# Weights ahead of the small value loads, bf16 masks, zero products and an earlier list: the opening of a fused attention and gated FFN kernel

## Chip, cores and metric

The kernel runs on one core of a Trainium2 chip. The metric is the device time of one launch in microseconds (us). Three runs of the kernel before took 1149.44, 1150.88 and 1152.57; the median is 1150.88.

## What is computed

The input is q, k and v of 8 batches, 8 heads, 576 positions and 64 dimensions, and the weights of a gated FFN. The attention has two parts that are added: a coarse one over means of four positions, and a local one over a band of seven keys. The sum is normalised and goes through the FFN.

```python
def _attn_ref(q, k, v):
    ...
    q_d = q.reshape(B, H, Sd, factor, D).mean(axis=3)
    ...
    out_d = sm_attn(q_d, k_d, v_d)
    out_up = np.repeat(out_d, factor, axis=2)
    mask = np.abs(pos[:, None] - pos[None, :]) < factor
    scores = scale * np.matmul(q, k.transpose(0, 1, 3, 2))
    scores = np.where(mask, scores, -1000000000.0)
    ...
    return (out_up + out_local).astype(np.float32)

def _moe_ref(x, w_gate, w_val, w_out, rms_g):
    rms = np.sqrt(np.mean(x * x, axis=-1, keepdims=True) + 1e-06)
    xn = x / rms * rms_g
    g = xn @ w_gate
    silu = g * (1.0 / (1.0 + np.exp(-g)))
    val = xn @ w_val
    return (silu * val @ w_out).astype(np.float32)
```

There are 4608 tokens of 512 features, and the FFN is 1536 wide. The weights arrive as 64-bit floats.

## The kernel before

The tokens go in 18 chunks of 256. Products on TensorE (PE) are made of two parts, a high and a low one, so a product of the FFN takes three matmuls.

**FFN of a chunk.** `Forward` goes through 12 slices f of 128 hidden features. The first step of a slice (L1323, 24 matmuls of 128x256) multiplies the normalised tokens xh and xl with w_gate and w_val. ACT takes the tanh (L1331), DVE makes the gate (L1334) and the product (L1339), ACT the high part (L1345), DVE or POOL the low part (L1348). The second step (L1359, 6 matmuls of 128x512) multiplies with w_out; it runs two slices behind the first.

**Local attention of a chunk c.** From c = 2 on it is `Attention`: eight pairs of score product (L786) and score sum (L790) on DVE, a softmax (L807 to L824), value products on ACT (L833), POOL and DVE (L840) with a sum on DVE (L859), the addition of the coarse part (L868, L874), squares (L884), the mean on PE (L891), the norm on DVE (L923), a turn on PE (L935), and the high and low part of the turned tokens (L940, L944), with which chunk c's FFN can start. For c = 0 and 1 it is `Dense`: masked scores on PE (the mask by an identity product L1089, the scores L1103), a softmax (L1118 to L1139), turns (L1145, L1156), values (L1166), the coarse part (L1178 for chunk 0; for chunk 1 loaded with L1188 and added with L1193), squares (L1205), the norm (L1235, L1237), the turn (L1247), the high part (L1250) and the low part (L1254). Its values come with `load_v`, 72 small transfers of v (L1072 of up to 16x512 elements, L1080 smaller).

**Coarse attention.** It goes in pieces: scores (L521), peak on DVE (L531), exps on ACT (L541), turn on PE (L550), copies on ACT (L558), values on PE (L565), scaling on DVE (L579) and a store to memory that ACT issues (L582). Eight pieces stand in the opening, the others beside the later chunks. Their sums over four positions come by a load on SP (L356, L360) and adding transfers of POOL (L364).

**Weights.** They come in 36 pieces of 512 KB. Each is fetched by SP (L251), scaled on ACT (L255), its last bits are taken on POOL (L265), both are joined on DVE (L272), the high part is made on ACT (L282, L284) and the low part split off on DVE (L294, L296) or POOL (L292). The fetches go to a few buffers that are used in turn, so a fetch waits until the piece before it in its buffer is joined.

**Order.** `Plan` (L66 to L160) is a list scheduler: tasks have an engine, a cost, a due time and buffers, and where several tasks could start on an engine at about the same time the one that is due first goes first. With it the opening is written out, from the first load to the last product of chunk 0's FFN, all weight pieces among it. Everything behind it comes from a loop over c = 1 to 17: it emits chunk c's FFN and between its slices the steps of chunk c + 1's attention, and the tile scheduler places these instructions, also between those of the opening. Each engine executes its instructions in the order that results. The transfers that SP and ACT issue share eight completion semaphores, and a transfer waits for the one before it on its semaphore.

Of the kernel before, what the change touches and what calls it, by code (L numbers as in the profile page):

```python
# [41 lines left out]
FIRST = 1  # L42
PIECES = {1: (0, 3, 6), 2: (0, 3, 6), 3: (0, 2)}
# [126 lines left out]
def attn_moe_kernel(  # L170
# [439 lines left out]
    class Attention:  # L610


        def __init__(self, c, na=4, np_=2, on_tensor=None):
            self.c, self.na, self.np, self.pt = c, na, np_, on_tensor
            self.x, self.qk, self.v, self.pr, self.y, self.up = {}, {}, {}, {}, {}, {}

        def steps(self):
# [46 lines left out]
            todo = [(0.37 * i, lambda i=i: score(i)) for i in range(8)] + [(3.0, softmax)]  # L664
# [4 lines left out]
        def plan(self, newton="POOL", before=()):  # L669
            c, np_, on_tensor, T = self.c, self.np, self.pt, due[self.c]  # L670
            early = c == 0
            sc, r = buf("sc"), buf("rms")
            xs, ups = [buf("x_t") for _ in range(2)], [buf("up_t") for _ in range(2)]
            self.xh_buf, self.xl_buf = buf("xh"), buf("xl")
            tps = [buf("ps_a") for _ in range(2)]

            loaded, k_bufs, last = {}, {}, []
            for n, jp in enumerate(jps):
                k_bufs[jp] = buf("kv"), buf("sil" if early and n > 1 else "q_t")
                loaded[jp] = task(  # L680
                    "SP", 0.15, lambda jp=jp: self.load_score(*jp), T - 88 + 7 * n - (200 if early else 0), allocs=k_bufs[jp],
                    dma=0.448 * MB,
                )
            for i, (j, par, s0) in enumerate(trio):
                at = T - 70 + 3.6 * i
                pr = buf("prod")
                p = task(
                    "DVE", 1.1, lambda i=i: self.score(i), at, [loaded[j, par]],
                    allocs=[pr] + ([sc] if i == 0 else []), uses=[*k_bufs[j, par], sc],
                )  # L690
                last.append(task("DVE", 1.08, lambda i=i: self.score_sum(i), at + 0.1, [p, *last[-1:]], uses=[pr, sc]))

            at = T - 40
            t = task("DVE", 0.5, self.peak, at, last, uses=[sc])
            t = task("DVE", 0.27, self.less, at, [t], uses=[sc])
            t = task("ACT", 0.3, self.powers, at, [t], uses=[sc])
            t = task("DVE", 0.26, self.total, at, [t], uses=[sc])
            t = task("DVE", 0.42, self.invert, at, [t], uses=[sc])
            shares = task("DVE", 0.27, self.shares, at, [t], uses=[sc])

            v_loaded, v_bufs, made = {}, {}, []
            for n, jp in enumerate(jps):
                v_bufs[jp] = buf("kv")
                v_loaded[jp] = task(
                    "SP", 0.1, lambda jp=jp: self.load_value(*jp), T - 55 + 7 * n - (60 if early else 0), allocs=[v_bufs[jp]],
                    dma=0.32 * MB,
                )
            self.y_bufs = [buf(on_tensor[1]) for _ in range(2)] if on_tensor else []
            for i, (j, par, s0) in enumerate(trio):
                at = T - 38 + 2.8 * i  # L710
                pr = buf("prod")
                first = task(
                    "ACT", 0.25 * self.na, lambda i=i: self.value_scalar(i, 0), at, [shares, v_loaded[j, par]],
                    allocs=[pr], uses=[v_bufs[j, par], sc],
                )
                parts = [first, task(
                    "ACT", 0.25 * self.na, lambda i=i: self.value_scalar(i, 1), at, with_=[first], uses=[pr, v_bufs[j, par], sc],
                )]
                for e, o0, o1, cost in (
                    ("DVE", self.na, NO - np_, 0.2 + 0.13 * (NO - np_ - self.na)), ("POOL", NO - np_, NO, 0.1 + 0.38 * np_),  # L720
                ):
                    if o0 < o1:
                        parts.append(task(
                            e, cost, lambda i=i, e=e, o0=o0, o1=o1: self.value(i, e, o0, o1), at, with_=[first],
                            uses=[pr, v_bufs[j, par], sc],
                        ))
                x0 = par == s0 == 0
                if on_tensor:
                    made.append(task(
                        "PE", 0.22 * NO, lambda i=i: self.value_sum(i), at - TAIL, [*parts, *made[-1:], *before],  # L730
                        allocs=[self.y_bufs[j]] if x0 else [], uses=[pr, self.y_bufs[j]],
                    ))
                else:
                    made.append(task(
                        "DVE", 1.07, lambda i=i: self.value_sum(i), at + 0.5, [*parts, *made[-1:]],
                        allocs=[xs[j]] if x0 else [], uses=[pr, xs[j]],
                    ))
            self.made = made

            up_ready = [stored[b, hp] for p_ in {(2 * c + j) // UPP for j in range(2)} for b in (2 * p_, 2 * p_ + 1) for hp in range(KT)]  # L740
            squares, adds = [], []
            for j in range(2):
                load = task("ACT", 0.12, lambda j=j: self.load_up(j), T - 30, up_ready, allocs=[ups[j]], lag=2.5)
                add = task(
                    "DVE", 0.69, lambda j=j: self.add_up(j), T - 18 + 3 * j, [made[4 * j + 3], load],
                    allocs=[xs[j]] if on_tensor else [], uses=[ups[j], xs[j], *([self.y_bufs[j]] if on_tensor else [])],
                )
                adds.append(add)
                squares.append(task("ACT", 1.1, lambda j=j: self.squares(j), T - 18 + 3 * j, [add], uses=[ups[j], xs[j]]))
            self.added = adds  # L750
            mp = buf("ps_a")
            mean = task("PE", 0.2, self.mean, T - 10 - TAIL, squares, allocs=[mp])
            rms = task("DVE", 0.48, self.rms, T - 10, [mean], allocs=[r], uses=[mp])
            root = task(newton, 2.6 if newton == "POOL" else 1.9, lambda: self.root(newton), T - 10, [rms], uses=[r])
            self.turned, self.turns = [], []
            for j in range(2):
                norm = task("DVE", 0.69, lambda j=j: self.norm(j), T - 8, [root], uses=[xs[j]])
                turn = task(
                    "PE", 0.6, lambda j=j: self.turn(j), T - 7 - TAIL, [norm],
# [718 lines left out]
    for b in q_bufs:  # L1478
        b.users.extend(atts[1].turns[:1])
    for n in range(len(pieces)):  # L1480
        decode(n)
# [109 lines left out]
```

## Time and profile before

| | us |
|---|---|
| profiled execution | 1153.86 |
| its span, first to last instruction | 1152.1 |
| median of three runs | 1150.88 |
| chunk 0's first FFN matmul (L1323) | 123.7 |
| chunk 0's output copies (L1367) begin | 234.3 |
| chunk 1's output copies begin | 293.6 |
| PE busy, over the span | 1053.5 |
| DVE busy | 908.7 |
| mean granted clock of PE | 0.948 |

A view of stretches has a row for each piece of time: the busy time of each engine with its number of instructions, PE's granted clock as a share of full speed, the share of time that the 16 transfer engines were busy, and the rate of transfers. A view of waits has the engine, the line that waited, what it waited for, and then the total, the number of times and the longest. A group of instructions has its line, engine, operation, names and shapes, the number, the busy time and the mean duration in ns, and the idle time before it. A row on one line gives the shortest, median and longest duration in ns and the first and last start. PEld is PE's loading of weights, which lies beside its matmuls; SPq is SP's own queue.

### The profile page before, as it was taken

How to read it: one execution, taken by the hardware profiler on the slowest of the kernel's cores; microseconds unless marked ns; L12 is line 12 of the kernel's file. 1: busy time of each engine (PE TensorE's matmuls, PEld its weight loads, DVE VectorE, ACT ScalarE, POOL GpSimd, SP SyncE). 2: the span in 40 equal slices, each digit the busy share in tenths (PEclk: the TensorE clock that was granted, in tenths of full speed). 3: DMA queues.
4: the chain of work that ended last, by engine and by line, in shares of the span. 5: the costliest groups of instructions: out<-in, count | busy, mean ns of one | idle time of the engine just before them, and what ended most of it. 6: DMA issues, size and time to landing. Idle time of an engine off the chain costs nothing.

```text
span 1152.1 us, 22708 instructions
## 1 busy us (share of the span) xinstructions
PE 1053.5 (91%) x8256; PEld 963.7 (84%) x8256; DVE 908.7 (79%) x1874; ACT 611.7 (53%) x2237; POOL 225.0 (20%) x279
## 2 busy tenths in 40 slices
PE   4285665799999999999999999999999999999998
PEld 3164554789999899999999999999999999999997
DVE  5246989736969898989898888888898989897432
ACT  3145477335556566474847474737374563837222
POOL 4122533602221213030312121101010010101000
PEclk9556687899999999999999999999999999999999
DMA  8356624832645444535353535322221313220000
GB/s 255 120 177 198 240 65 128 181 80 41 157 89 125 95 120 92 129 73 133 79 128 83 131 85 123 91 68 71 68 89 46 106 52 99 67 59 20 1 19 19
DMA packets 74172, 115.28 MB, mean 100 GB/s; under 512 B 26204, under 2 KB 34652, under 8 KB 74060
## 3 DMA queue, kind: packets, MB, share of 16 engines
q1 hardware_dynamic: 45484, 93.15, 26.6%
q0 software_dynamic: 8640, 15.93, 8.9%
q10 hardware_dynamic: 19936, 4.76, 1.9%
q8 instruction: 65, 1.06, 0.4%
q14 instruction: 47, 0.39, 0.1%
HBM read 102.00 MB, written 11.80 MB: 99 GB/s over the span
## 4 chain that ended last, share of the span: by engine, by line
PE 81%; DMA 7%; DVE 5%; SPq 3%; ACT 2%; issue 1%; POOL 1%; ACTq 0%; DVEq 0%; POOLq 0%
PE ps_h L1323 49%; PE ps_o L1359 25%; PE ps_a L565 2%; SPq L1072 2%; DMA wg<-in_v_sum_dram 2%; DMA qk<-in_qk_sum_dram 2%; PE ps_a L521 1%; PE ps_a L935 1%; PE ps_a L550 1%; ACT prod L833 1%; DVE prod L786 1%; DVE o_sb L272 1%; DMA wv<-in_w_val_dram 1%; DVE sc L790 1%; DMA up_t<-up 1%
## 5 line engine op out<-in xcount | busy, mean ns | idle before, releaser
L1359 PE MATMUL ps_o<-wo,hs 128*128 128x512 f32 x1296 | 340.5, 401 | 11.6 <-DVE hs L1348 7.5
L1323 PE MATMUL ps_h<-xh,wg 128*128 128x256 f32 x1728 | 319.2, 281 | 1.4 <-DVE wg L296 1.4
L1323 PE MATMUL ps_h<-xh,wv 128*128 128x256 f32 x1728 | 316.7, 280 | 0.0
L1323 PEld LDWEIGHTS ps_h<-xh,wg 128*128 128x128 f32 x1728 | 268.0, 190 | 10.3 <-issue 3.3
L1359 PEld LDWEIGHTS ps_o<-wo,hs 128*128 128x128 f32 x1296 | 231.6, 190 | 51.6 <-DVE hs L1348 8.4
L833 ACT ACTIVATE prod<-kv,sc 128x64 f32<-128x64 f32 x1024 | 262.4, 406 | 20.7 <-DMA up<-o_g 7.7
L1323 PEld LDWEIGHTS ps_h<-xh,wv 128*128 128x128 f32 x1728 | 268.4, 191 | 2.9 <-issue 0.4
L1323 PE MATMUL ps_h<-xl,wv 128*128 128x256 f32 x864 | 242.8, 281 | 19.9 <-DVE sil L1334 18.1
L1323 PE MATMUL ps_h<-xl,wg 128*128 128x256 f32 x864 | 244.3, 283 | 0.1
L1331 ACT ACTIVATE sil<-ps_h 128x256 f32<-128x256 f32 x216 | 81.5, 378 | 235.3 <-PE ps_h L1323 219.5
L1323 PEld LDWEIGHTS ps_h<-xl,wv 128*128 128x128 f32 x864 | 165.0, 191 | 24.2 <-DVE sil L1334 20.3
L1323 PEld LDWEIGHTS ps_h<-xl,wg 128*128 128x128 f32 x864 | 164.2, 190 | 7.2 <-DVE sil L1339 0.9
L840 POOL TENSOR_TENSOR prod<-sc,kv 128x256 f32<-128x256 f32 x128 | 96.2, 789 | 375.6 <-DVE sc L824 161.5
L859 DVE TENSOR_REDUCE x_t<-prod 128x128 f32<-128x896 f32 x128 | 136.2, 1074 | 31.1 <-PE ps_a L935 27.8
L1345 ACT ACTIVATE hs<-sil 128x256 fp32r<-128x256 f32 x216 | 89.2, 414 | 133.7 <-DVE sil L1339 104.5
L1334 DVE SCALAR_TENSOR_TENSOR sil<-sil,ps_h 128x256 f32<-128x256 f32 x216 | 88.9, 412 | 66.7 <-ACT sil L1331 64.2
L786 DVE TENSOR_TENSOR prod<-q_t,kv 128x896 f32<-128x896 f32 x128 | 140.5, 1100 | 0.1
L790 DVE TENSOR_REDUCE sc<-prod 128x14 f32<-128x896 f32 x128 | 136.9, 1073 | 0.0
L1348 DVE TENSOR_TENSOR hs<-sil,hs 128x256 fp32r<-128x256 f32 x209 | 97.2, 468 | 30.6 <-ACT hs L1345 30.0
L1339 DVE SCALAR_TENSOR_TENSOR sil<-sil,ps_h 128x256 f32<-128x256 f32 x216 | 89.6, 415 | 2.3 <-PE ps_h L1323 0.8
L364 POOL DMA_DIRECT2D qk<-in_qk_sum_dram x36 | 32.7, 907 | 250.0 <-DMA qk<-in_qk_sum_dram 207.9
L541 ACT ACTIVATE a_g<-ps_a,m_g 72x144 f32<-72x144 f32 x112 | 40.5, 370 | 38.9 <-DMA kv<-in_v_sum_dram 25.5
(169 smaller groups left out, 928.1 us busy)
## 6 DMA issues: line engine op xcount, KB each, us to landing
kv<-in_k_pad_dram SPq DMA_DIRECT2D x64, 320.0 KB
kv<-in_v_pad_dram SPq DMA_DIRECT2D x64, 320.0 KB
qk<-in_qk_sum_dram POOLq DMA_DIRECT2D x36, 288.0 KB, 5.0
out_dram<-o_sb SPq DMA_DIRECT2D x36, 256.0 KB
q_t<-in_q_band_dram SPq DMA_DIRECT2D x64, 128.0 KB
vs<-in_v_sum_dram POOLq DMA_DIRECT2D x36, 144.0 KB, 3.3
qk<-in_qk_sum_dram SPq DMA_DIRECT2D x12, 288.0 KB
wo<-in_qk_sum_dram SPq DMA_DIRECT2D x2, 1152.0 KB
```

The costliest lines, as they stand in the source:

```text
L786: nc.vector.tensor_tensor(out=pr, in0=bcast(q[:, s0:s0 + 2], 2, NO), in1=window(k, s0), op=ALU.mult)
L790: nc.vector.tensor_reduce(out=self.sc[:, j, par, s0:s0 + 2], in_=self.pr[i], axis=AX.X, op=ALU.add,)
L833: nc.scalar.activation(out=self.pr[i][:, o, s], in_=self.v[j, par][:, s0 + s + o], func=AF.Copy, scale=p[:, s, o:o + 1],)
L840: (nc.vector if engine == "DVE" else nc.gpsimd).tensor_tensor(out=self.pr[i][:, a:b], in0=bcast(p[:, :, a:b].rearrange("p s o -> p o s"), ...
L859: nc.vector.tensor_reduce(out=self.x[j][:, s0:s0 + 2, par], in_=pr.rearrange("p o s d -> p s d o"), axis=AX.X, op=ALU.add,)
L1323: last = nc.tensor.matmul(out=self.p[f][:, t], lhsT=wi(f)[:, 0, k], rhs=xi[:, k], start=(n == 0), stop=(n == 3 * KT - 1),).ins
L1331: nc.scalar.activation(out=self.sil[f], in_=self.p[f][:, 0], func=AF.Tanh, scale=0.5)
L1334: nc.vector.scalar_tensor_tensor(out=self.sil[f], in0=self.sil[f], scalar=1.0, in1=self.p[f][:, 0], op0=ALU.add, op1=ALU.mult,)
L1339: nc.vector.scalar_tensor_tensor(out=self.sil[f], in0=self.sil[f], scalar=0.5, in1=self.p[f][:, 1], op0=ALU.mult, op1=ALU.mult,)
L1345: nc.scalar.activation(out=self.hs[f][:, 0], in_=self.sil[f], func=AF.Copy)
L1348: (nc.gpsimd if engine == "POOL" else nc.vector).tensor_tensor(out=self.hs[f][:, 1], in0=self.sil[f], in1=self.hs[f][:, 0], op=ALU.subtract,)
L1359: last = nc.tensor.matmul(out=self.o[j], lhsT=lhs[:, cols], rhs=rhs(f)[:, 0], start=(f == 0 and i == 0), stop=(f == NF - 1 and i == 2),).ins
```

## The change

1. **Transfers.** The due times of `load_v` change, so that SP issues the first eight weight pieces ahead of the 72 small transfers of v.
2. **Masks.** The masks and the identity that brings them into the scores become bf16, for which POOL makes a bf16 copy of the identity; the costs of the dense scores and values in the list become smaller.
3. **Zero products.** Up to 100 products of a zero matrix (bf16, 128x256) are offered to the list for PE, due last, so that they stand where the list has PE free. They add nothing to their accumulator. Those that fall behind chunk 0's squares are not issued: 28 are.
4. **Scores of the third chunk.** `Attention.plan`, which nothing used, is removed; `plan_scores` puts the third chunk's (c = 2) key loads, score pairs and softmax into the list, due from 130 on, and the loop leaves them out.

```diff
-                        "SP", 0.25, lambda b=b, e=e: self.load_v(b, e), (-80 if early else 45) + 2 * b + e,
+                        "SP", 0.25, lambda b=b, e=e: self.load_v(b, e), (50.0 if early else 53.5) + 0.1 * (2 * b + e),
...
-                    "PE", 3.4 if b == 0 else 2.6, lambda b=b: self.scores(b), at + 2 * b,
+                    "PE", 1.8 if b == 0 else 0.9, lambda b=b: self.scores(b), at + 2 * b,
...
+                for i in range(IDLE):
+                    task("PE", 0.13, self.idle, 1e6 + i, first, not_before=20.0 + 0.3 * i)
...
-                        out=self.s[par].rearrange("p b t a k -> p (b t a) k"), lhsT=ident_sb,
+                        out=self.s[par].rearrange("p b t a k -> p (b t a) k"), lhsT=masks["ident"],
...
+        def idle(self):
+            if not hasattr(self, "ss"):
+                nc.tensor.matmul(
+                    out=self.x[0][:, 0].rearrange("p h d -> p (h d)"), lhsT=masks["zero"], rhs=bcast(masks["ident"], 1, 2),
+                    start=False, stop=True, skip_group_check=True,
+                )
...
+        masks["ident"] = t.bitcast(BF16)[:, 2 * D:2 * D + P]
+        nc.gpsimd.tensor_copy(out=masks["ident"], in_=ident_sb)
+        masks["zero"] = t.bitcast(BF16)[:, 6 * D:8 * D]
+        nc.gpsimd.memset(masks["zero"], 0.0)
...
+        def plan_scores(self, at):
+            self.scored = True
...
+                loaded[jp] = task(
+                    "SP", 0.4, lambda jp=jp: self.load_score(*jp), at - 20 + 5 * n, allocs=k_bufs[jp], dma=0.448 * MB,
+                )
+            for i, (j, par, s0) in enumerate(trio):
...
+                    "DVE", 1.1, lambda i=i: self.score(i), at + 3 * i, [loaded[j, par]],
...
+    early = Attention(2).plan_scores(130.0)
     for n in range(len(pieces)):
         decode(n)
...
-            nxt = Attention(c + 1)
+            nxt = early if c == FIRST else Attention(c + 1)
```

The rows below are the instructions of one engine in the order in which they stand, those of the changed kernel with its own line numbers. On SP, behind the loads of the sums, before the change (L1072 and L1080 are the small transfers of v, L251 the weights):

```order
L1072 DMA kv<-in_v_sum_dram 12x1x512
L1072 DMA kv<-in_v_sum_dram 16x1x512 x3
L1080 DMA kv<-in_v_sum_dram 4x4x64 x2
L1072 DMA kv<-in_v_sum_dram 16x1x512 x8
L251 DMA wg_1_359<-in_w_gate_dram 128x1024
L251 DMA wg_1_359<-in_w_val_dram 128x1024
```

The same place in the changed kernel (L252 is L251, L1001 is L1072, L1009 is L1080):

```order
L252 DMA wg_1_296<-in_w_gate_dram 128x1024
L252 DMA wg_1_296<-in_w_val_dram 128x1024
L252 DMA wg_1_328<-in_w_out_dram 128x1024
L252 DMA wg_1_328<-in_w_gate_dram 128x1024
L252 DMA wv_1_358<-in_w_val_dram 128x1024
L252 DMA wv_1_358<-in_w_out_dram 128x1024
L252 DMA wv_1_392<-in_w_gate_dram 128x1024
L252 DMA wv_1_392<-in_w_val_dram 128x1024
L1001 DMA kv<-in_v_sum_dram 12x1x512
L1001 DMA kv<-in_v_sum_dram 16x1x512 x3
```

Before, 40 small transfers of chunk 0 stand ahead of the first weight; now eight weights stand ahead of the first small one.

On DVE, behind chunk 0's low parts, before the change (L272 joins, L296 splits, L786 and L790 score pairs, L1334 gate):

```order
L296 SCALAR_TENSOR_TENSOR wv_0_861<-o_sb,g_sb,wv_0_860 128x4x128
L786 TENSOR_TENSOR prod<-q_t,kv 128x896 x2
L272 SCALAR_TENSOR_TENSOR o_sb<-o_sb,wv_1_434 128x512 x2
L272 SCALAR_TENSOR_TENSOR o_sb<-o_sb,wv_1_521 128x512
L790 TENSOR_REDUCE sc<-prod 128x14 x2
L1334 SCALAR_TENSOR_TENSOR sil<-sil,ps_h 128x256
L296 SCALAR_TENSOR_TENSOR wg_0_527<-o_sb,g_sb,wg_0_526 128x4x128
L786 TENSOR_TENSOR prod<-q_t,kv 128x896
```

In the changed kernel the first score pair (L712, L716) stands far behind, after the splits (L297) and joins (L273) of nearly all pieces (L1270 is the gate, L1275 the product, L1284 the low part):

```order
L273 SCALAR_TENSOR_TENSOR o_sb<-o_sb,wo_2_587 128x512
L297 SCALAR_TENSOR_TENSOR wv_1_1517<-o_sb,g_sb,wv_1_1516 128x4x128
L712 TENSOR_TENSOR prod<-q_t,kv 128x896
L716 TENSOR_REDUCE sc<-prod 128x14
L712 TENSOR_TENSOR prod<-q_t,kv 128x896
L1270 SCALAR_TENSOR_TENSOR sil<-sil,ps_h 128x256 x2
L273 SCALAR_TENSOR_TENSOR o_sb<-o_sb,raw 128x512
L1275 SCALAR_TENSOR_TENSOR sil<-sil,ps_h 128x256
```

Of the 36 joins all but two stand ahead of the first score; before, the scores of the third and of the fourth chunk stand between them. The fourth chunk's scores stand behind the third's in both.

On PE the zero products that stand close together are those between the scores and the turn of the eighth coarse piece. Before:

```order
L1178 MATMUL ps_o<-o_g,q_t 64x128 x2
L521 MATMUL ps_h<-xl 72x144 x4
L550 MATMUL ps_h<-ident_sb,a_g 72x72 x8
L1145 MATMUL ps_a<-ident_sb,wo_1_865 128x128 x4
L565 MATMUL ps_h<-hs,a_g 72x64 x8
```

In the changed kernel (L1107 is L1178, L1114 the zero product, L522 is L521; 18 more zero products follow the last row here, and then the turn):

```order
L1107 MATMUL ps_o<-o_g,q_t 64x128 x2
L1114 LDWEIGHTS q_t
L1114 MATMUL ps_o<-q_t 128x256
L522 MATMUL ps_h<-xl 72x144 x4
L1114 LDWEIGHTS q_t
L1114 MATMUL ps_o<-q_t 128x256
```

The first scores of the ninth coarse piece (L521, with the first sums that POOL adds) stand on PE behind chunk 1's slice 4 (16 first steps and 12 second steps of chunks 0 and 1 are ahead of them); before, 14 and a third first steps and 11 second steps are.

More of the change, by code (lines that the diff above doesn't have):

```diff
@@ L42 @@
 FIRST = 1
+IDLE = 100
 PIECES = {1: (0, 3, 6), 2: (0, 3, 6), 3: (0, 2)}
@@ L613, in __init__ @@
         def __init__(self, c, na=4, np_=2, on_tensor=None):
-            self.c, self.na, self.np, self.pt = c, na, np_, on_tensor
+            self.c, self.na, self.np, self.pt, self.scored = c, na, np_, on_tensor, False
             self.x, self.qk, self.v, self.pr, self.y, self.up = {}, {}, {}, {}, {}, {}
@@ L662, in turn @@
                 return last
-            todo = [(0.37 * i, lambda i=i: score(i)) for i in range(8)] + [(3.0, softmax)]
+            todo = [] if self.scored else [(0.37 * i, lambda i=i: score(i)) for i in range(8)] + [(3.0, softmax)]
             todo += [(3.1 + 0.42 * i, lambda i=i: value(i)) for i in range(8)]
@@ L667, in steps @@
             return todo, root, turn
[L669 to L675, printed above, removed]
+        def plan_scores(self, at):
+            self.scored = True
+            sc = buf("sc")
@@ L677, in plan @@
             loaded, k_bufs, last = {}, {}, []
             for n, jp in enumerate(jps):
-                k_bufs[jp] = buf("kv"), buf("sil" if early and n > 1 else "q_t")
+                k_bufs[jp] = buf("kv"), buf("q_t")
                 loaded[jp] = task(
-                    "SP", 0.15, lambda jp=jp: self.load_score(*jp), T - 88 + 7 * n - (200 if early else 0), allocs=k_bufs[jp],
-                    dma=0.448 * MB,
+                    "SP", 0.4, lambda jp=jp: self.load_score(*jp), at - 20 + 5 * n, allocs=k_bufs[jp], dma=0.448 * MB,
@@ L683, in plan @@
                 )
             for i, (j, par, s0) in enumerate(trio):
-                at = T - 70 + 3.6 * i
                 pr = buf("prod")
                 p = task(
-                    "DVE", 1.1, lambda i=i: self.score(i), at, [loaded[j, par]],
+                    "DVE", 1.1, lambda i=i: self.score(i), at + 3 * i, [loaded[j, par]],
                     allocs=[pr] + ([sc] if i == 0 else []), uses=[*k_bufs[j, par], sc],
                 )
-                last.append(task("DVE", 1.08, lambda i=i: self.score_sum(i), at + 0.1, [p, *last[-1:]], uses=[pr, sc]))
@@ L693, in plan @@
[L693 to L759, printed above, removed]
-                    allocs=[tps[j]] + ([self.xh_buf, self.xl_buf] if j == 0 else []), uses=[xs[j], self.xh_buf, self.xl_buf],
-                )
-                high = task("ACT", 0.58, lambda j=j: self.high(j), T - 7, [turn], uses=[tps[j], self.xh_buf])
-                low = task("DVE", 0.69, lambda j=j: self.low(j), T - 7, [high], uses=[tps[j], self.xh_buf, self.xl_buf])
-                self.turned += [high, low]
-                self.turns.append(turn)
+                last.append(task("DVE", 1.08, lambda i=i: self.score_sum(i), at + 3 * i, [p, *last[-1:]], uses=[pr, sc]))
@@ L766, in plan @@
+            t = last
+            for e, cost, f in (
+                ("DVE", 0.5, self.peak), ("DVE", 0.27, self.less), ("ACT", 0.3, self.powers), ("DVE", 0.26, self.total),
+                ("DVE", 0.42, self.invert), ("DVE", 0.27, self.shares),
+            ):
+                t = [task(e, cost, f, at + 24, t, uses=[sc])]
             return self
@@ L1014, in plan @@
                 values.append(task(
-                    "PE", 2.8, lambda par=par: self.values(par), end - 15 + par,
+                    "PE", 1.2, lambda par=par: self.values(par), end - 15 + par,
                     [copies[par], *v_ready, *values[-1:], *(first if early else [p.valued for p in pieces])],
@@ L1033, in plan @@
             self.valued = values[-1:]
+            if early:
+                for i in range(IDLE):
+                    task("PE", 0.13, self.idle, 1e6 + i, first, not_before=20.0 + 0.3 * i)
             x_ts = [buf("x_t") for _ in range(2)]
@@ L1453, in make_masks @@
         for c in range(2):
-            masks[c] = t[:, c * D:(c + 1) * D]
+            masks[c] = t.bitcast(BF16)[:, c * D:(c + 1) * D]
             nc.gpsimd.tensor_scalar(
```

## Prediction

> **What bounds the kernel now.** I read the page's head first, then the stretches of the span, then where four milestones lie.
>
> ```profile
> span 1152.1 us, 22708 instructions
> PE 1053.5 (91%) x8256; PEld 963.7 (84%) x8256; DVE 908.7 (79%) x1874; ACT 611.7 (53%) x2237; POOL 225.0 (20%) x279
> ```
>
> The stretches give the busy time of PE, PEld, DVE, ACT, POOL, then the granted clock.
>
> ```profile
> 120.00:150.00 30.00, 22.33 (x112) 19.36 (x113) 30.00 (x39) 13.65 (x29) 15.42 (x14) 0.78 0.59 202
> 150.00:180.00 30.00, 22.52 (x122) 19.73 (x121) 26.35 (x55) 25.40 (x74) 12.01 (x14) 0.83 0.24 74
> 180.00:210.00 30.00, 15.35 (x83) 13.70 (x84) 29.75 (x42) 17.55 (x58) 10.82 (x10) 0.77 0.48 147
> 210.00:240.00 30.00, 24.94 (x175) 22.82 (x174) 15.33 (x35) 12.35 (x42) 14.37 (x17) 0.94 0.82 160
> 240.00:270.00 30.00, 30.00 (x245) 27.39 (x245) 12.45 (x42) 8.94 (x32) 5.17 (x6) 1.00 0.36 62
> ```
>
> From 240 us on PE is full at clock 1.00, so only what comes earlier can change. From 120 to 210 DVE is full and PE has holes; from 210 to 270 DVE is half idle. The milestones, each the first start of its line:
>
> ```profile
> L1235 DVE TENSOR_SCALAR x_t<-ps_o,rinv x2: 473/478/482, 109.2 to 109.6; 128x256 f32<-128x256 f32 x2
> L1323 PE MATMUL ps_h<-xl,wg x864: 276/276/583, 123.7 to 1142.4; 128*128 128x256 f32 x173
> L923 DVE TENSOR_TENSOR x_t<-x_t,rinv x32: 682/686/692, 270.1 to 1085.4; 128x512 f32<-128x512 f32 x32
> L944 DVE TENSOR_TENSOR xl<-ps_a,xh x32: 678/680/703, 279.3 to 1091.7; 128x512 fp32r<-128x512 f32 x32
> ```
>
> Chunk 0's norm is at 109.2, its FFN starts at 123.7, chunk 2's norm is at 270.1 and its xl starts at 279.3; its two parts of 0.68 end near 281, when chunk 2's FFN starts. After that both kernels hold the same work (chunk 3's scores are done by then in both), on a full PE. So the change is worth what it moves the 281. What PE waited for between 120 and 240 (total, times, longest):
>
> ```profile
> PE ps_h L1323 <- DVE sil L1334: 18.1, 7, 4.5
> PE ps_a L1193 <- DMA raw<-up: 8.3, 1, 8.3
> PE ps_o L1359 <- DVE hs L1348: 7.5, 2, 5.7
> PE ps_o L1359 <- POOL hs L1348: 4.1, 2, 2.1
> PE ps_a L521 <- DMA qk<-in_qk_sum_dram: 2.0, 1, 2.0
> ```
>
> **The scores, the largest part.** DVE works in the order in which it is told. Before, chunk 2's and chunk 3's 16 score pairs stand between the weight joins, so chunk 0's gates (L1334) and low parts (L1348) come late, and PE with them: 18.1 + 7.5 = 25.6 us. The groups of DVE between 107 and 270:
>
> ```profile
> L786 DVE TENSOR_TENSOR prod<-q_t,kv 128x896 f32<-128x896 f32 x16 | 19.5, 1232 | 0.0
> L790 DVE TENSOR_REDUCE sc<-prod 128x14 f32<-128x896 f32 x16 | 16.8, 1072 | 0.0
> L1334 DVE SCALAR_TENSOR_TENSOR sil<-sil,ps_h 128x256 f32<-128x256 f32 x21 | 8.7, 414 | 17.8 <-ACT sil L1331 16.0 <-PE ps_h L1323 1.8
> ```
>
> After, the first score stands behind all joins but two: 19.5 + 16.8 = 36.3 us of DVE leave the stretch in which PE waits and fill the one in which DVE idles. DVE's two stretches around it:
>
> ```profile
> 107.00:210.00 103.00, 62.17 (x323) 54.36 (x324) 97.70 (x156) 62.66 (x171) 43.46 (x41) 0.76 0.49 156
> 210.00:281.00 71.00, 65.94 (x510) 60.69 (x509) 34.77 (x90) 26.42 (x91) 20.97 (x25) 0.98 0.51 96
> ```
>
> DVE has 97.7 + 34.8 = 132.5 us of work in these 174 us and the change keeps all of it. So DVE alone allows chunk 2's FFN at 107 + 132 = 239. For PE: its stretch from 123.7 to 281 is 157 us long, less 25.6 for the waits on DVE is 132, which gives 256 with the clock as it is. I expect 20 of the 25.6 to go; 5.6 stay, because joins, splits and gates still share one engine and each weight must still be fetched.
>
> **The clock** follows PE's holes: with 22.33 busy of 30 it was 0.78, with 24.94 it was 0.94, with 30 it was 1.00. PE is busy 62.17 us from 107 to 210 at 0.76, which is 62.17 × 0.24 = 15 us of half-speed excess. With two thirds of the waits gone I take 5 off (estimate; bounds 0 and 10).
>
> **What is late next: the sums for the ninth coarse piece.** PE stands at L521 for them, and behind it in PE's order are chunk 1's last products and chunk 2's mean and turn.
>
> ```profile
> L251 SPq DMA_DIRECT2D raw<-in_w_out_dram x2: 328/331/334, 197.6 to 205.3; - x2
> ```
> ```profile
> 211.64 4.45 DMA qk<-in_qk_sum_dram
> 216.44 7.38 DMA qk<-in_qk_sum_dram
> ```
> ```profile
> 232.32 0.71 PE L521 MATMUL ps_a<-qk 64*72 64x144 f32 x8 [1.96 <-DMA qk<-in_qk_sum_dram]
> ```
>
> The last weight fetch is at 205.3; 27 us later (two SP loads, POOL's adding DMAs L364) L521 runs; 49 us after that, at 281, comes chunk 2. By the new order 8 of chunk 1's first steps stand behind L521 instead of 9.67, and one second step fewer. A first step is 24 matmuls, a second 6:
>
> ```profile
> 248.71 2.75 PE ps_h L1323 x24
> 863.21 2.75 PE ps_o L1359 x12
> ```
>
> That is 1.67 × 2.75 + 1.37 = 6 us less, so 43 behind L521. The last fetch needs the raw buffer of the piece before it, which DVE's joins free. Before the last joins DVE has some 36 us less to do, at 107 in place of 109; with 10 us of new idle it comes some 28 us earlier, near 178, L521 near 205, and chunk 2 could start at 248. With none of this it is 205 + 27 + 43 = 275. Against the sum over PE's waits (below, 258) this term decides only if the fetch comes after about 188; nothing is added. But chunk 2's values, mean, root and turn now follow its scores closely. DVE idled 71 − 35 = 36 us between 210 and 281, mostly ahead of L923; of such cover at most 258 − 107 − 132 = 19 us is left in all. I add 3 us of PE waiting for that chain (bounds 0, and the 9.2 us from L923 to L944 in full).
>
> **Transfers.** SP's issues ahead of the first weights, the first stretch, and what ACT waited for up to 110:
>
> ```profile
> 13.23 4.19 SPq L1072 DMA_DIRECT2D kv<-in_v_sum_dram  x4
> ...
> 50.13 0.45 SPq L251 DMA_DIRECT2D wg<-in_w_gate_dram  x1
> ...
> 52.59 7.63 SPq L1072 DMA_DIRECT2D wo<-in_v_sum_dram  x6
> ```
> ```profile
> 0.00:30.00 30.00, 14.39 (x212) 9.64 (x212) 17.77 (x29) 11.13 (x37) 15.33 (x28) 1.00 0.80 247
> ```
> ```profile
> ACT a_g L541 <- DMA kv<-in_v_sum_dram: 25.5, 1, 25.5
> ACT a_g L541 <- DMA wo<-in_v_sum_dram: 6.1, 1, 6.1
> ...
> ACT o_sb L255 <- DMA wg<-in_w_gate_dram: 5.2, 1, 5.2
> ACT o_sb L255 <- DMA wg<-in_w_val_dram: 2.7, 1, 2.7
> ```
>
> Eight weights (4.2 MB) go at 13 instead of 50; at 247 GB/s they take 17 us, behind the loads under way. The small ones stand behind them on SP, and ACT's stores (L582), which share completion semaphores with SP's transfers, wait for them: that is ACT's 25.5 us, with the exps (L541) queued behind the store. I expect this wait to end some 9 us later (loads till about 30, weights till 47, then a small one). Later waits shrink: the 6.1, and 5.2 + 2.7 for the first weights' scaling (L255), 14 us in all; by the last opening piece the 9 are made up. Chunk 0's norm comes at 107, between 103 and 116. I take −2.
>
> The Trainium skill, "DMA: Bandwidth & Descriptors" (Queues, rings and completion order), says that each DMA engine takes one queue's descriptors in ring order and takes turns between SP's and ACT's queues. By that alone ACT's stores would pass the weights, the 9 us would not arise and the opening would gain up to 7 more; the row of 25.5 us, which puts ACT's wait on a transfer of SP, speaks against it.
>
> **Masks and idle products.** PE around the eighth coarse piece:
>
> ```profile
> 82.64 3.78 PE L1089 MATMUL ps_h<-q_t,ident_sb 128*128 128x512 f32 x4
> ...
> 95.03 1.42 PE L550 MATMUL ps_h<-ident_sb,a_g 72*72 72x72 f32 x8 [2.40 <-ACT a_g L541]
> ```
> ```profile
> 95.00:100.00 5.00, 4.85 (x35) 4.26 (x35) 4.09 (x11) 2.07 (x7) 0.00 (x0) 0.52 0.00 0
> ```
>
> The masks' four products in bf16 go at L1359's 0.23 us each at full clock, 0.46 at half: 1.8 in place of 3.78, 2 us less. Chunk 1's softmax follows them, not chunk 0's norm: 0 to −2, I take 0. Between L521 and L550 now stand 19 zero products of 128x256. One takes 2.75/24 = 0.115, or 0.23 at half clock: 2.2 to 4.4 us. Their cover is the 2.40 wait for the exps; beyond it they cost up to 2 us on the path to the norm. I take +1. POOL's copy of the identity and the memset lie in the opening's first 30 us, in which POOL is busy 15.33: nothing.
>
> **Sum.** −20 (waits for DVE) −5 (clock) +3 (chunk 2's chain) −2 (opening) +1 (zero products) = −23: chunk 2 at 258. The profiled execution took 1153.9 (1152.1 and 1.8 around it), so 1131; the median of the runs shown, 1150.9, is 3 less, and on it the time is **1128**. With all terms at their good ends it is −25.6 − 10 − 2 = −38; with half of the 25.6, no clock, 6 for the chain, the opening as it was and +2 for the products it is −5.
>
> **Rivals.**
> (a) *The sums hold chunk 2 back.* Fetches, not joins, set the pace: the stretch from 120 to 150 already moved 202 GB/s. Against it, 180 to 210 moved 147 and 150 to 180 only 74. If the last fetch comes at 195, chunk 2 starts at 195 + 27 + 43 + 3 = 268: 13 us gained, **1138**; with the fetch unmoved 278, which is (d). Chance 0.25.
> (b) *PE alone bounds.* DVE's waits and half the clock's excess go entirely and chunk 2's chain is covered: −35, **1116**. That is −25.6, −7.5 and −2. For it: DVE's floor of 239 lies lower. Against: FFN and joins alternate on one engine. 0.12.
> (c) *Slower: the small transfers hold the opening.* ACT's first store is late by 9 and each later small one by as much, since SP issues the 72 behind eight weights; nothing is made up, chunk 0's norm comes at 121, the fetches that wait for its buffers come 12 late and the last one at 217, and chunk 2 starts at 217 + 27 + 43 + 3 = 290: +9, **1160**. It decides from a last fetch later than 208 + 3.5. For it: the 25.5 us wait. Against: ACT's second half had 14 us of waits to give. 0.07.
> (d) *Nothing to see*: the fetch falls at 205 to 211 and eats the gain, within 3.5 us. 0.05. That the change doesn't do what it says is excluded by the order, apart from the zero products, of which only 28 of 100 are issued.
> (e) *The zero products lift the clock.* From 95 to 100 PE was busy 4.85 us at 0.52. At full clock that is 2.5 us: −2 in place of the +1, and **1125**. Against it: those 4.85 busy microseconds did not lift the clock themselves. The Trainium skill, "TensorE: Matmul & The Clock Gate" (Part 1: The HAM clock gate), says that about 3.4 us of sustained activity brings the full clock. The 0.52 does not agree with it. Chance 0.08.
>
> The forecast, gains of 15 to 31 without (e), has 0.43. A measurement of this kernel can tell about 0.3%, 3.5 us, from no change. Range: 1114 (just beyond b) to 1146 (all of a but its worst end): (c), (d) and the ends beyond leave out less than 0.2. Faster 0.88, same 0.05, slower 0.07.
>
> **What would show it.** Right: waits of L1323 and L1359 on DVE under 10 us before chunk 2, DVE full on to about 240, L944 first near 257, the last raw fetch before 188, L1235 first within 103 to 111, L541's long wait over near 55. Wrong: L521 waiting over 5 us for the sums (a); L1235 first after 116 (c); chunk 2's L923 with PE idle over 9 us ahead of its FFN; or a period after chunk 2 that is not that of before.

## The result and the profile after

The changed kernel took 1134.65 us (median of 4 runs, 1132.48 to 1135.05) against 1151.72 for the kernel before (4 runs); the ratio is 0.9845, 95% interval 0.9817 to 0.9874. The profiled execution took 1134.34 with a span of 1132.6, against 1153.86 and 1152.1: 19.5 us less, where 23 were forecast; between the medians it is 17.1. The line numbers of the changed kernel differ: L1259 is the FFN's first step (L1323 before), L1295 the second (L1359), L1270 the gate (L1334), L1284 the low part (L1348), L712 and L716 the score pairs, L273 the joins (L272), L522 the coarse scores (L521), L849 the norm (L923), L861 the turn (L935), L870 the low part of xl (L944).

The stretches of the changed kernel, with the busy time of PE, PEld, DVE, ACT and POOL, then the granted clock:

```profile
120.00:150.00 30.00, 25.62 (x181) 23.67 (x181) 25.20 (x48) 20.65 (x47) 16.51 (x17) 0.96 0.22 76
150.00:180.00 30.00, 24.83 (x154) 21.49 (x153) 27.16 (x40) 15.63 (x31) 14.49 (x14) 0.94 0.63 195
180.00:210.00 30.00, 22.86 (x166) 21.55 (x165) 20.03 (x41) 11.18 (x40) 15.63 (x19) 0.89 0.81 172
210.00:240.00 30.00, 30.00 (x245) 27.28 (x244) 25.24 (x45) 20.24 (x86) 6.53 (x8) 1.00 0.47 105
240.00:270.00 30.00, 22.40 (x149) 19.23 (x149) 27.99 (x66) 20.92 (x88) 10.39 (x11) 0.89 0.47 110
```

Between 120 and 210 PE is busy 73 us of 90 where it was 60, at clocks of 0.89 to 0.96. A new hole stands between 240 and 270, where PE had been full. The milestones, by the first start in each row:

```profile
L1171 DVE TENSOR_SCALAR x_t<-ps_o,rinv x2: 476/480/485, 105.4 to 105.8; 128x256 f32<-128x256 f32 x2
L1259 PE MATMUL ps_h<-xl,wg x864: 276/276/582, 117.6 to 1122.8; 128*128 128x256 f32 x173
L849 DVE TENSOR_TENSOR x_t<-x_t,rinv x32: 683/689/2215, 253.1 to 1065.8; 128x512 f32<-128x512 f32 x32
L870 DVE TENSOR_TENSOR xl<-ps_a,xh x32: 680/681/684, 257.9 to 1072.2; 128x512 fp32r<-128x512 f32 x32
```

Chunk 0's norm came 3.8 us earlier, its FFN 6.1, chunk 2's xl 21.4; the span is 19.5 shorter, so 1.9 us were given back behind chunk 2. What PE waited for between 115 and 270:

```profile
PE ps_a L861 <- DVE x_t L849: 7.3, 1, 7.3
PE ps_a L522 <- DMA qk<-in_qk_sum_dram: 6.1, 1, 6.1
PE ps_o L1295 <- DVE hs L1284: 4.0, 2, 2.7
PE ps_h L1259 <- DVE sil L1270: 4.0, 3, 1.6
PE ps_o L1295 <- POOL hs L1284: 2.1, 2, 1.1
```

The waits on DVE inside the FFN fell from 25.6 to 8.0 us. In their place PE waits 7.3 us for chunk 2's norm and 6.1 for the ninth coarse piece's sums.

### The profile page after: what moved, and what is told of

The parts are those of the page before. It is cut to its first block, busy times and chain, and to the rows that moved or that the text cites. A ratio compares the mean times of both kernels' runs of the same rounds, so it can differ in the third digit from the quotient of the medians.

```text
span 1132.6 us, 22791 instructions
## 1 busy us (share of the span) xinstructions
PE 1045.1 (92%) x8278; PEld 960.0 (85%) x8278; DVE 907.3 (80%) x1869; ACT 611.6 (54%) x2237; POOL 228.6 (20%) x286
## 4 chain that ended last, share of the span: by engine, by line
PE 79%; DMA 8%; DVE 6%; issue 2%; ACT 2%; SPq 1%; POOL 1%; ACTq 0%; DVEq 0%; POOLq 0%
PE ps_h L1259 47%; PE ps_o L1295 23%; PE ps_a L566 2%; DMA qk<-in_qk_sum_dram 2%; DMA wg<-in_v_sum_dram 2%; PE ps_a L522 1%; PE ps_a L861 1%; DVE prod L712 1%; PE ps_a L551 1%; DVE sc L716 1%; DMA wv<-in_w_val_dram 1%; DMA up<-o_g 1%; SPq L1001 1%; DVE o_sb L273 1%; DMA wo<-in_qk_sum_dram 1%
## 5 line engine op out<-in xcount | busy, mean ns | idle before, releaser
L1295 PE MATMUL ps_o<-wo,hs 128*128 128x512 f32 x1296 | 339.1, 400 | 6.1 <-DVE hs L1284 4.0
L1259 PE MATMUL ps_h<-xh,wg 128*128 128x256 f32 x1728 | 318.7, 281 | 0.0
L1259 PE MATMUL ps_h<-xh,wv 128*128 128x256 f32 x1728 | 311.6, 277 | 0.0
L1259 PEld LDWEIGHTS ps_h<-xh,wg 128*128 128x128 f32 x1728 | 268.3, 191 | 7.7 <-issue 2.7
L1295 PEld LDWEIGHTS ps_o<-wo,hs 128*128 128x128 f32 x1296 | 231.2, 190 | 45.8 <-DVE hs L1284 4.7
L1259 PEld LDWEIGHTS ps_h<-xh,wv 128*128 128x128 f32 x1728 | 264.5, 188 | 2.8
L1259 PE MATMUL ps_h<-xl,wg 128*128 128x256 f32 x864 | 245.3, 284 | 0.1
L1259 PE MATMUL ps_h<-xl,wv 128*128 128x256 f32 x864 | 240.3, 278 | 4.5 <-DVE sil L1270 4.0
L1259 PEld LDWEIGHTS ps_h<-xl,wg 128*128 128x128 f32 x864 | 164.8, 191 | 7.8 <-issue 1.8
L1259 PEld LDWEIGHTS ps_h<-xl,wv 128*128 128x128 f32 x864 | 162.6, 188 | 8.2 <-DVE sil L1270 5.6
L712 DVE TENSOR_TENSOR prod<-q_t,kv 128x896 f32<-128x896 f32 x128 | 139.7, 1093 | 0.1
L716 DVE TENSOR_REDUCE sc<-prod 128x14 f32<-128x896 f32 x128 | 137.6, 1077 | 0.0
L1270 DVE SCALAR_TENSOR_TENSOR sil<-sil,ps_h 128x256 f32<-128x256 f32 x216 | 89.3, 414 | 55.1 <-ACT sil L1267 50.7
L1284 DVE TENSOR_TENSOR hs<-sil,hs 128x256 fp32r<-128x256 f32 x207 | 98.6, 478 | 29.4 <-ACT hs L1281 29.0
L1275 DVE SCALAR_TENSOR_TENSOR sil<-sil,ps_h 128x256 f32<-128x256 f32 x216 | 90.1, 417 | 4.8 <-PE ps_h L1259 3.6
L766 DVE TENSOR_TENSOR prod<-sc,kv 128x128 f32<-128x128 f32 x128 | 54.8, 450 | 0.9
```

Of the source, the lines that this page charges most:

```text
L712: nc.vector.tensor_tensor(out=pr, in0=bcast(q[:, s0:s0 + 2], 2, NO), in1=window(k, s0), op=ALU.mult)
L716: nc.vector.tensor_reduce(out=self.sc[:, j, par, s0:s0 + 2], in_=self.pr[i], axis=AX.X, op=ALU.add,)
L766: (nc.vector if engine == "DVE" else nc.gpsimd).tensor_tensor(out=self.pr[i][:, a:b], in0=bcast(p[:, :, a:b].rearrange("p s o -> p o s"), ...
L1259: last = nc.tensor.matmul(out=self.p[f][:, t], lhsT=wi(f)[:, 0, k], rhs=xi[:, k], start=(n == 0), stop=(n == 3 * KT - 1),).ins
L1270: nc.vector.scalar_tensor_tensor(out=self.sil[f], in0=self.sil[f], scalar=1.0, in1=self.p[f][:, 0], op0=ALU.add, op1=ALU.mult,)
L1275: nc.vector.scalar_tensor_tensor(out=self.sil[f], in0=self.sil[f], scalar=0.5, in1=self.p[f][:, 1], op0=ALU.mult, op1=ALU.mult,)
```

## The experiments

All ratios are of the kernel named to the kernel before, each with its 95% interval; that of the changed kernel is 0.9845.

### Which part brought it

**The scores alone.** The kernel before with the third chunk's scores placed by the list:

```diff
+    early = Attention(2).plan_scores(130.0)
...
-            nxt = Attention(c + 1)
+            nxt = early if c == FIRST else Attention(c + 1)
```

> The kernel before with the third chunk's scores placed by the list alone: small v transfers first, masks in f32, no zero products. Theory A (the order of the scores on DVE is the main part): chunk 0's norm stays near 109, PE's waits for DVE between 120 and 260 fall from 25.6 us to under 10, and the time falls by 11 to 16 us, to 1136 to 1141. Theory B (the weights' earlier transfers are the main part): without them the joins come as late as before, the waits for DVE or for weights stay above 18 us, and the time is within 4 us of 1151.

It took 1134.97, ratio 0.9846 (0.9825 to 0.9867): as fast as the whole change, and 1 us better than theory A's bounds. Chunk 0's norm comes at 108.0, and PE's waits for the gates and low parts of DVE are 4.4 + 2.2 us, under the 10 that theory A named. Theory A holds, theory B falls, and beside the scores the rest of the change adds up to nothing.

**All but the scores.** The changed kernel without those lines:

> The changed kernel with the third chunk's scores left to the scheduler as before; transfers, masks and zero products changed. Theory A: FFN of chunk 0 starts near 118 as in the changed kernel, but the scores stand between the joins again, PE waits for DVE by 18 to 26 us, and only the opening's 4 to 6 us are gained: 1145 to 1148. Theory B: the weights are there early, so most of the gain stays: 1134 to 1139.

It took 1158.74, ratio 1.006 (1.0038 to 1.0083): neither theory, though the waits for DVE that theory A named are there. The weights' early transfers don't help, and the three other parts together cost time. PE's waits in this run between 100 and 300:

```profile
PE ps_h L1259 <- DVE sil L1270: 14.3, 6, 4.9
...
PE ps_o L1295 <- DVE hs L1284: 9.2, 2, 5.1
PE ps_o L1295 <- POOL hs L1284: 6.4, 4, 3.7
```

The 14.3 + 9.2 us on DVE are those of the kernel before (25.6), and POOL's 4.1 became 6.4. Its chunk 0's norm starts at 112.0, later than in both kernels. The trace shows two holds ahead of it: ACT stops for 5.6 us between chunk 0's squares, which the view puts to a weight's transfer, and on DVE two score pairs of the third chunk (5.2 us from 104.4 on) stand between the steps of chunk 0's root. No run separates the two.

**The transfers as before.** The changed kernel with the small v transfers first:

```diff
-                        "SP", 0.25, lambda b=b, e=e: self.load_v(b, e), (50.0 if early else 53.5) + 0.1 * (2 * b + e),
+                        "SP", 0.25, lambda b=b, e=e: self.load_v(b, e), (-80 if early else 45) + 2 * b + e,
```

> The changed kernel with the small v transfers ahead of the weights again; scores, masks and zero products changed. Theory A: it keeps the gain of the scores and loses 2 to 6 us in the opening: 1136 to 1141. Theory B: it loses most of the gain, 1146 to 1152.

It took 1128.04, ratio 0.978 (0.9755 to 0.9805). Both theories expected a loss; it is 6.6 us faster than the changed kernel. The transfers ahead of the small ones cost time. What the prediction saw of it is there: ACT's first store, by the first start of its row in the changed kernel,

```profile
L583 ACTq DMA_DIRECT2D up<-o_g x32: 298/310/822, 50.4 to 804.6; - x32
```

waited until 50.4 where it had been 42.2 (in the run with the small transfers first it is 41.9), since 72 small transfers start behind eight weights:

```profile
13.20 0.41 SPq L252 DMA_DIRECT2D wg<-in_w_gate_dram  x1
...
30.11 0.33 SPq L252 DMA_DIRECT2D wv<-in_w_val_dram  x1
31.12 4.39 SPq L1001 DMA_DIRECT2D kv<-in_v_sum_dram  x4
```

The delay of 8.2 us is not lost directly: chunk 0's norm came at 105.4 all the same. What differs between the two runs is the stretch from 80 to 105. First the changed kernel, then the run with the small transfers first:

```profile
80.00:105.00 25.00, 15.89 (x410) 11.98 (x408) 15.58 (x37) 12.13 (x33) 6.55 (x8) 0.84 0.62 203
```
```profile
80.00:105.00 25.00, 16.15 (x267) 12.40 (x265) 24.00 (x53) 18.12 (x50) 10.53 (x12) 0.86 0.79 273
```

DVE works 24.0 us there instead of 15.6 and the transfers move 273 GB/s instead of 203: by its order 12 joins stand ahead of chunk 0's norm on DVE, in the changed kernel 7, before 8. From 105 to 120 DVE then has 7.6 us to do instead of 15.0.

**The masks, and the zero products.** Two runs take the zero products out, one of the changed kernel, one of the run just told:

```diff
-IDLE = 100
+IDLE = 0
```

> The changed kernel without the zero products. Theory A (they lift the clock in the opening): the products behind the eighth coarse piece run at about half speed again, chunk 0's norm comes 2 to 4 us later than 105.4, and the time is 1136 to 1139. Theory C (they do nothing or cost up to 2 us): norm within 1 us of 105.4, time 1132 to 1135.

> The list's scores and the bf16 masks, with the small v transfers first and no zero products. Theory D (the zero products keep PE's clock up in the opening): chunk 0's norm, 101.7 with them, comes at 104 to 107, the time is 1130 to 1134. Theory E (the bf16 masks made the opening faster, by shorter products and by the list's other order): norm within 1.5 us of 101.7 and the time within 2 us of 1128.

They took 1133.93, ratio 0.9837 (0.9806 to 0.9868), and 1130.15, ratio 0.9796 (0.9769 to 0.9824). With and without the products the intervals overlap (0.9845 and 0.9837; 0.978 and 0.9796): they are worth about 2 us at most. For the changed kernel theory C holds by the time; its norm, 1.3 us later, just misses C's 1 us. In the other run theory D holds: its norm is 5.5 us later, 0.2 beyond D's bound, and the time is within D's. Its trace with them has 40 zero products, that of the changed kernel 26. Chunk 0's norm and the stretch from 80 to 105 with the small transfers first and no zero products:

```profile
L1171 DVE TENSOR_SCALAR x_t<-ps_o,rinv x2: 473/478/482, 107.2 to 107.6; 128x256 f32<-128x256 f32 x2
```
```profile
80.00:105.00 25.00, 14.88 (x212) 11.39 (x212) 18.50 (x42) 16.09 (x46) 10.54 (x11) 0.52 0.76 262
```

The clock there is 0.52 instead of 0.86 with them. So the zero products do bring chunk 0's norm forward in that order, by 5.5 us, and only about 2 of these are left in the time. In the changed kernel they hold up the clock locally. PE at the eighth coarse piece, in the changed kernel:

```profile
88.57 2.25 PE L1114 MATMUL ps_o<-q_t 128*128 128x256 bf16 x19
91.71 0.44 PE L551 MATMUL ps_h<-ident_sb,a_g 72*72 72x72 f32 x4 [0.89 <-ACT a_g L542]
```

and without them:

```profile
92.14 1.41 PE L551 MATMUL ps_h<-ident_sb,a_g 72*72 72x72 f32 x8 [3.84 <-ACT a_g L542]
```

The 19 products fill a gap of 3.84 us; behind it the same turn runs at 0.11 us a product with them and at 0.18 without. But chunk 0's norm moves only from 106.7 to 105.4. The Trainium skill, "TensorE: Matmul & The Clock Gate" (Part 1: The HAM clock gate), says that the clock goes to half after an idle window of about 3.4 us; the gap of 3.84 with slow products behind it agrees, and the gap of 0.89 with fast ones too. The gap alone does not decide the speed: in the run with the small transfers first and no zero products the turn is slow (1.41 us for its 8 products, at 90.7) behind a gap of 0.78, in the stretch of clock 0.52.

The masks are left: scores alone 0.9846 (0.9825 to 0.9867), scores and masks 0.9796 (0.9769 to 0.9824), 4.8 us less between the medians, by intervals that just don't meet. The list is given smaller costs with them, and 12 joins instead of 8 stand ahead of chunk 0's norm. With the scores alone, chunk 1's mask products (four of 0.95 us, from 83.1 on) stand on PE between the steps of the last coarse pieces; in bf16 they are two of 0.63 us, which the list puts near 59. PE's last coarse product ahead of chunk 0's norm then starts at 95.7 instead of 101.3, but the norm itself only at 107.2 instead of 108.0. Whether the shorter products or the list's other order brings the gain no run here separates.

### A step of PE that was not the cause

In the runs with 12 early joins, chunk 1's products of the coarse part (add_rows, L1129; L1193 before) also stand behind four first steps of chunk 0's FFN. In the changed kernel they stand ahead of the first, with 6.0 us of waiting for their load. Three runs put only them behind such steps, by a time before which the list doesn't take them:

```diff
-                ups = [task("PE", 1.6, self.add_rows, end - 12, [t, *values], uses=[up, *x_bufs])]
+                ups = [task("PE", 1.6, self.add_rows, end - 12, [t, *values], uses=[up, *x_bufs], not_before=85.0)]
```

> The changed kernel, with only chunk 1's four products of the coarse part (add_rows) put behind four first steps of chunk 0's FFN instead of ahead of the first. Theory J (the place of these products, with their wait for a load, makes the changed kernel slower than the one with the small transfers first, where they stand behind four steps too): chunk 0's FFN starts near 112 instead of 117.6 and the time is 1127 to 1130. Theory K (the weights ahead of the small transfers cost it, by ACT's stores): the start moves but the joins do not, and the time is 1133 to 1136.

> The list's scores alone (masks in f32, small transfers first, no zero products), with chunk 1's products of the coarse part behind four first steps. Theory J: chunk 0's FFN starts near 114 instead of 120.5, and the time falls from 1135 to 1128 to 1131. Theory E (the bf16 masks themselves make the opening faster): 1133 to 1136.

> The kernel before, with only chunk 1's products of the coarse part behind four first steps of chunk 0's FFN. Its joins are held up by DVE's scores: if DVE sets chunk 0's pace there (theory A), an earlier start of PE by 6 us is lost again and the time stays within 3 us of 1152. Theory J alone, without regard to DVE: 1144 to 1147.

From the changed kernel it took 1132.89, ratio 0.9819 (0.9788 to 0.985); from the scores alone 1134.37, 0.9833 (0.9804 to 0.9862); from the kernel before 1153.43, 1.0006 (0.9987 to 1.0026). Theory J falls in all three; the second lies in theory E's range and the third in theory A's, and the first is 0.1 us better than theory K's bounds. Chunk 0's FFN does start earlier, first in the changed kernel so edited, then in the kernel before:

```profile
L1259 PE MATMUL ps_h<-xl,wg x864: 276/276/582, 109.9 to 1123.5; 128*128 128x256 f32 x173
```
```profile
L1323 PE MATMUL ps_h<-xl,wg x864: 276/276/583, 115.6 to 1142.5; 128*128 128x256 f32 x173
```

That is 7.7 and 8.1 us, and nearly all of it is gone at chunk 2: its xl starts at 258.6 against 257.9, and at 278.5 against 279.3. In the changed kernel so edited the lead is gone by the first second step: from the start of chunk 0's FFN to that step it takes 17.3 us (109.9 to 127.2) instead of 9.3 (117.6 to 126.9). PE waits 4.0 of these, 2.4 for weights that ACT and DVE have not made yet and 1.6 for a gate, and its clock is 0.53 instead of 0.73. An early start of PE is worth about 2 us at most here. The time goes with the early joins: of the runs so far that have the list's scores, the two with 12 early joins took 1128.0 and 1130.2, those with 7 or 8 from 1132.9 to 1135.0. No run moves the joins alone.

### The two new waits

All of these have the small transfers first. **The sums.** Chunk 1's coarse pieces go later:

```diff
-PIECES = {1: (0, 3, 6), 2: (0, 3, 6), 3: (0, 2)}
+PIECES = {1: (4, 6, 8), 2: (0, 3, 6), 3: (0, 2)}
```

> Small v transfers first, and chunk 1's three coarse pieces later: the first one's scores stand on PE behind one more first step and three more second steps, 6.9 us. Theory H (the wait for the sums, 6.2 us, is on the path): it falls below 1 us, DVE, which waited for the same scores, goes on, and the time falls by 3 to 6, to 1122 to 1125. Theory I (DVE's work sets chunk 2's norm, the wait only moves): PE waits as much more ahead of chunk 2's turn, and the time is 1126.5 to 1129.5.

It took 1122.52, ratio 0.9728 (0.9703 to 0.9753), 5.5 us under the run with small transfers first, by intervals that just don't meet. PE's wait for the sums is gone from its view. Theory H holds: the wait for the sums was on the path. The reason is that DVE stands in it too. DVE in the changed kernel:

```profile
204.24 0.45 DVE L532 TENSOR_REDUCE m_g<-ps_a 72x2 f32<-72x288 f32 x1 [6.38 <-PE ps_a L522]
```

The peak of the coarse scores comes before chunk 2's value sums in DVE's order, so while PE waited for the sums, DVE lost 6.4 us of the work that sets chunk 2's norm.

**Chunk 2's norm.** In the changed kernel the fourth chunk's scores stand on DVE between the steps of chunk 2's root. Two runs put them behind its norm, all eight, or the last three with the softmax:

```diff
...
-                todo.pop(0)[1]()
+                with behind(att.normed if c == FIRST + 1 and todo[0][0] >= 0.0 else None):
+                    todo.pop(0)[1]()
```

(1.8 instead of 0.0 for the last three; `att.normed` is the norm's second instruction.)

> Small v transfers first, and all of the fourth chunk's scores on DVE behind chunk 2's norm. Theory F (what PE waits for ahead of chunk 2's FFN, 7.3 us, is the fourth chunk's scores between the steps of chunk 2's root): the wait falls below 3 us, chunk 2's xl starts near 249, the time is 1121 to 1125. Theory G (the work is only put off: 17 us of DVE then lie in chunk 2's FFN): PE waits 5 us or more for chunk 3's norm, and the time is 1126 to 1131.

> As the run before it, but only the last three of the fourth chunk's scores and its softmax stand behind chunk 2's norm. Theory F: the wait ahead of chunk 2's FFN falls to about 3 us, and chunk 3's norm is in time since 7 us are put off instead of 17: 1122 to 1126. Theory G: 1127 to 1130.

They took 1134.97, ratio 0.9839 (0.9812 to 0.9866), and 1125.73, 0.976 (0.9733 to 0.9787), against 0.978. Chunk 2's xl did start earlier, at 245.7 and 243.0 instead of 254.4, and PE's wait for chunk 2's norm fell from 7.3 us to 0.5 and 0.3: to this point theory F holds, and the scores were what PE waited for. The lead was given back one chunk later. The stretch from 290 to 320, first of the run with the small transfers first, then all eight behind the norm, then three:

```profile
290.00:320.00 30.00, 30.00 (x235) 26.89 (x235) 25.08 (x63) 19.57 (x74) 10.11 (x13) 1.00 0.55 106
```
```profile
290.00:320.00 30.00, 17.99 (x113) 16.24 (x112) 28.39 (x60) 11.52 (x47) 5.70 (x8) 0.77 0.54 117
```
```profile
290.00:320.00 30.00, 22.52 (x147) 19.93 (x146) 23.84 (x59) 16.19 (x63) 8.97 (x11) 0.89 0.49 104
```

PE waits 12.0 and 7.5 us there, 8.3 and 4.6 of them for chunk 3's norm and the rest for steps of DVE behind it; at clocks of 0.77 and 0.89 its 18.0 and 22.5 busy us hold another 4.1 and 2.5 of slow excess. For all eight this is theory G's mechanism, but the time is 4 us beyond its range. For three the time lies in theory F's range, but chunk 3's norm was not in time as F had it: the gain and what was given back are about the same, and 0.976 can't be told from 0.978.

**Both together**, the later coarse pieces and the last three scores behind the norm:

> Small v transfers first, the other parts of the change, chunk 1's coarse pieces later (6.9 us more PE work ahead of the first) and the last three of the fourth chunk's scores behind chunk 2's norm. If the waits for the sums and for chunk 2's norm are independent, the two gains add: 1120 to 1122. If the second gain was already lost to chunk 3's later norm: 1122 to 1125.

It took 1123.53, ratio 0.9747 (0.972 to 0.9775). That is no better than the later coarse pieces alone (0.9728); the second expectation holds. Chunk 2's xl starts at 234.9, 11.4 us ahead of that run's 246.3, and its stretch from 290 to 320 shows where it went:

```profile
290.00:320.00 30.00, 22.71 (x146) 19.96 (x145) 24.34 (x62) 16.81 (x68) 9.86 (x12) 0.89 0.45 96
```

The fastest version by its median is the changed kernel with the small v transfers first and chunk 1's coarse pieces later, 0.9728; the one with both can't be told from it.

## Why the prediction came out as it did

The time on record, 1128 with 1114 to 1146, holds the measured 1134.65, and the main mechanism was right: the scores' place on DVE. That chunk 2 came at 259.2, where 258 was forecast, is in part luck. DVE's waits fell by 2.4 us less than forecast, chunk 2's chain cost 4.3 more, and the sums 4.1 more: together 10.8 us too few. Chunk 0's FFN started 5.1 us earlier than the −2 and +1 of the sum allow, and waits of PE for POOL, ACT and split weights, which the sum leaves out, fell by 4.5. Most of the 6.7 us between 1128 and 1134.65 is the 1.9 us given back behind chunk 2 and the 3 us by which the forecast went down from the profiled execution to the median: the changed kernel's profiled execution lies at its median. By the steps:

**Waits for DVE, −20.** Measured 25.6 to 8.0, −17.6. The run with the scores alone shows that this part carries the whole gain, and the run without them that nothing is left.

**Clock, −5.** In the stretch from chunk 0's first step to chunk 2's, first before, then after:

```profile
123.70:280.60 156.90, 122.10 (x811) 110.59 (x811) 116.78 (x218) 80.35 (x246) 56.63 (x58) 0.88 0.46 116
```
```profile
117.60:259.20 141.60, 117.31 (x819) 105.98 (x819) 118.70 (x219) 78.44 (x242) 60.31 (x65) 0.92 0.53 136
```

122.10 × 0.12 = 14.7 us of slow excess became 117.31 × 0.08 = 9.4: −5.3. Right.

**Chunk 2's chain, +3, bounds 0 and 9.2.** Measured 7.3: mis-sized. I had asked how much idle time of DVE is left; I had not looked at what stands between mean and norm in DVE's new order. There the fourth chunk's scores stand between small steps: from the first step behind the mean (244.9) to the norm (253.1) it is 8.2 us, before the change it was 3.0, and with the scores put behind the norm it is 3.8 and 3.5.

**The sums, nothing unless the last fetch comes after 188.** This step failed. The fetch came early, but L522 still waited. First the fetch and the adding transfers of the changed kernel, then PE:

```profile
L252 SPq DMA_DIRECT2D raw<-in_w_out_dram x2: 327/328/328, 164.2 to 172.2; - x2
...
L365 POOL DMA_DIRECT2D qk<-in_qk_sum_dram x36: 856/886/1057, 179.2 to 693.8; - x36
```
```profile
203.00 1.24 PE L522 MATMUL ps_a<-qk 64*72 64x144 f32 x8 [6.07 <-DMA qk<-in_qk_sum_dram]
```

From fetch to L522 it took 30.8 us, not 27, and from L522 to chunk 2 56.2, not 43, with the 7.3 us for chunk 2's norm among them. And the forecast compared two ends of the sum for PE as if only the later counted; PE came to L522 at 197, so the wait was real, and DVE stood in it. It cost 6.1 − 2.0 = 4.1 us in this sum. The condition of rival (a), with its fetch at 195, did not occur, but the sign named for it (L521 waiting over 5 us) did, and so did its mechanism, chunk 2 held back by the sums: the run with the later coarse pieces shows it. DVE, which was to be full to about 240, worked 20.0 of the 30 us from 180 to 210.

**The opening, −2, with the zero products +1.** Chunk 0's norm at 105.4 lies in the 103 to 111 that were named. The delay of ACT's first store was to be 9 us and was 8.2, and it was made up, as forecast. But the reason for calling it a gain was wrong: the transfers cost 6.6 us, by the run that takes them back, and with the small transfers first 4.8 us come with the masks, to which the prediction gave 0 because chunk 0's norm does not follow them. The prediction asked only when chunk 0's norm and FFN come. The runs with the moved products show that this date is worth about 2 us at most; the time goes with how many weights DVE has joined by then, though that was not changed by itself.

**The zero products and rival (e).** They did hold the clock where they stand, and the 19 took 2.25 us inside a gap of 3.84, so they cost nothing. In the changed kernel they moved chunk 0's norm by 1.3 us, with the small transfers first by 5.5, and the time by no amount that can be told from none.

**Behind chunk 2, nothing.** The prediction took PE as full from there on. The changed kernel loses 1.9 us of its lead there, and the view of waits behind 259 has one row:

```profile
PE ps_a L817 <- ACT up_t L810: 2.5, 1, 2.5
```

It is the mean of a later chunk, at 366.9. That is the first sign of what the last runs showed at full size: chunk 2's start is not a fixed mark from which the rest takes its time.

Of the 19.5 us in the profiled executions, the start of chunk 0's FFN brings 6.1, PE's waits between there and chunk 2 some 10, the clock 5.3, less 1.9 behind.

## What to carry to other kernels

Where an engine that executes in order feeds another, count what stands on it ahead of each date, not only its idle time: the small steps of a chain (mean, root, norm) take as long as the long ones put between them. A lead that is made by putting work off has to be followed until the work is done; here 11 us of lead at chunk 2 came back as waiting and a lower clock at chunk 3. And the start of the bottleneck engine was worth little here, where what it needs next is made elsewhere at its own pace.

## What the runs showed of the hardware

In the changed kernel without zero products a gap of 3.84 us on PE was followed by products at 0.18 us each; with the zero products in the gap and 0.89 us of it left, the same products took 0.11. Where PE had been slow already, they took 0.18 behind a gap of 0.78. And with eight large loads put first on SP's queue, ACT's first store to memory was issued at 50.4 us instead of 41.9. In the Trainium skill's "DMA: Bandwidth & Descriptors" (Queues, rings and completion order) the DMA engines take turns between the two queues, and by that alone its issue would not have moved; the store's issue, not its transfer, waited.
